# A new order for TensorE in the first attention block, and later due times in the planner that writes it out

## The chip, the core and the metric

The kernel runs on one core of a Trainium2 chip, as one launch. The metric is device microseconds (us) from the launch's start to its end, the median of a few runs. A profile is one execution, recorded instruction by instruction by the hardware. The engines are TensorE (PE; its weight loads are PEld), VectorE (DVE), ScalarE (ACT) and GpSimd (POOL); SyncE (SP) issues nearly all transfers (DMA). Each engine works through its own instructions in the order in which they were written; semaphores tie the engines together.

## The reference

Two attention blocks with inputs of their own, results side by side. Both have 2048 rows, width 512, 32 heads of 16. Block A sees a sliding window of 256 keys, block B all keys.

```python
def _A_ref(x, wqkv, wo):          # _B_ref: the same without the mask
    qkv = (x @ wqkv).reshape(B, S, 3, H, Dh) -> q, k, v   # H = 32, Dh = 16
    scores = einsum("bhqd,bhkd->bhqk", q, k) * (Dh ** -0.5)
    mask = (i - j >= 0) & (i - j < 256)
    scores = where(mask, scores, -1e9)
    o = einsum("bhqk,bhkd->bhqd", softmax(scores), v)
    return concat_heads(o) @ wo
return concatenate([a, b], axis=-1)                # (1, 2048, 1024)
```

All is float32. The kernel reaches that accuracy with two rounded float32 tiles per operand, a rounded value and what it left over, and three products of them.

## The kernel before

**Units.** The work is cut into units (block, group of 4 heads, chunk of 512 queries): 8 groups by 4 chunks make 32 units in each block, numbered 0 to 31 for A and 32 on for B. Unit 19 is group 4, chunk 3 of A.

**The letters.** In block A the order of TensorE is a string, `ORDER_A`, one letter for one step:
- `p`: one projection, 12 matmuls with 128x512 results (`products`, L173), of queries or keys (`project_qk`) or values (`project_v`). ScalarE takes the result out of PSUM (L232, L236 or L312); for queries and keys VectorE or GpSimd makes the two parts (L242, L246, L247), SP stores them to DRAM (L254), and per group they are loaded again as `oq` (L300) and `opk` (L284). There are two store buffers for queries and keys and two for values. The projections of both blocks lie in this string, 96 of them.
- `m`: scores of two heads against a window of 384 keys (L407, 2 matmuls), for the row maximum alone. VectorE copies the masked part and takes the maximum (L416, L417); in the first two query tiles of chunk 0 it does so in another form (L412). Two PSUM buffers serve all m. A unit has 8 m; after the last one `max_finish` makes the negated maxima in three parts (L444 to L447 on VectorE).
- `t`: a transpose of those maxima (L455). ScalarE copies them out (L457) and its own queue sends them into three rows of `oq` (L462).
- `s`: scores of two heads, now less the maximum (L488); ScalarE takes the exponential out of PSUM (L495), GpSimd zeroes the masked corners (L505). A unit has 6 s. Three PSUM buffers serve s, shared with p.
- `w`: exponentials times values (L534), 3 per unit; after the last ScalarE copies the sums out (L545) and SP stores them (L552).
- `e`: maxima for the first unit of block B, against keys loaded early into the buffer of the values (L359; loads L376 and L384).

**The loads.** `load_split` loads a tile of x or of a weight through SP (L141) into a staging buffer. Later ScalarE copies it rounded (L126) and GpSimd, or VectorE for the first tiles, subtracts that from the original (L127). Tiles of the kind "stage" (all of block B, and weights of A but the first) have three staging buffers. A load is written when its condition holds and the planner finds its source ready.

**The planner.** `Model` keeps a time for each engine, for SP and for the transfers, and is run along while the instructions are written. It costs nothing on the chip: its times decide only in which order instructions stand in their engines' programs. The loop over `ORDER_A` asks for each letter when its operands are ready on that clock, and moves the clock there. What other engines do later is put off by `after(time, f)` and written when TensorE's model time passes that time (`settle`); `at_most` and `follow` write it earlier where a buffer or an operand asks for it. `LAND` is added to some of those times for transfers to arrive. `operands` says when a projection may start: its tiles split, and a store buffer free by the time it ends. `invert_now` loads the sums of a chunk (L566), takes reciprocals on VectorE (L571) and stores them (L573), for both blocks.

**Block B** follows a short pattern, `ORDER`, with 16 key tiles for each unit, paced by a fixed step; the same planner places its loads and output projections.

Of the kernel before, what the change touches and what calls it, by code (L numbers as in the profile page):

```python
# [50 lines left out]


ORDER_A = (
    "pppppppmmpmmpmpmpmmpmtmmpmsmmpmsmppmmtpmsmswsmmspmmswwspsmwtsmmpmswmmspsmmwsmptmmpsmmswmspmmspmmswsm"
    "mswtmmspmmswsmpsmwsmtmwmspmsmwsmpmsmwstmwmspsmmpmsmwspmsmwtsmpmmswsmpmsmwsmpmsmtwmsmpsmmswsmmpsmsmws"
    "wtmmspsmmwsmpsmmwsmtpsmmswmsmwsmptpmsmwswmmspmsmwmspmspmswsmsmtwmmspsmmwsmpsmmwstmwmsmpmswmssmmssmmt"
    "mwmsmsmwsmwmssmmswsmtmsmwmsmsmwsmpmmwsmmswsmtmpsmwmsmmswmmsmtpssmmpwstmsmmwmsmswsmmstwspwssmpmsmwmsm"
    "swmsmswmsmsmpmmwmtmswmmssmwsmsmpmsmwsmsmtwmsmpsmmtwspmmswsmwwsmmpsmwtmsmpmmswspmswmsmpmsmtwspsmwmspm"
    "smwsmpswsmmpmsmswtmmspsmwmsmpsmwsmmtpmswmsmwsmpeswespmswmmspeswsmmpmswtemspesmpesmpmsmwsmwsempesmwtm"
    "spesmwsmpestmwsmmpmsmwsmpeswmswemspemspesmtwsepmsmwsmpmswsempmsmwsmptmmwsmpmsmpwmmpsmmpmswsmmpmsmpsm"  # L60
    "mpmmpmmwwtpmm")
LAND = 700


class Model:
# [41 lines left out]
def attention_kernel(ctx: ExitStack, tc: tile.TileContext, xT, wqk, wv, wo, out):  # L107
# [9 lines left out]
    M = Model()  # L117
    ready = {}
# [11 lines left out]
    slots_st, slots_v = [0, 0], [0, 0]  # L130
    staged = {"stage": [0] * 3, "p": [0] * 2 * AHEAD}

    def load_split(srcs, tags, d, keys, stage):

        slots = staged[stage]
        bufs_in = 3 if stage == "stage" else 2 * AHEAD
        at_most(stage, bufs_in - 1)
        r = sb.tile([128, 512] if stage == "stage" else [128, 2, QC], F32, name=f"in_{keys[0]}".translate(NAMES),
                    tag=stage, bufs=bufs_in)
        r = r[:, None] if stage == "stage" else r[:, 0:len(keys)]  # L140
        nc.sync.dma_start(r, srcs)  # L141
        t = M.dma(256 * len(keys), slots.pop(0))

        def rest():
            for n, (tag, key) in enumerate(zip(tags, keys)):
                d[key] = split(r[:, n], tag[0], f"{key}".translate(NAMES), tag[1],
                               nc.gpsimd if stage == "stage" else nc.vector)
                ready[tag[0], *key] = M.run(*(("Pool", 1260) if stage == "stage" else ("DVE", 602)),
                                            M.run("ACT", 500, t))
            slots.append(ready[tag[0], *key])  # L150
        after(t + (LAND if stage == "stage" else 0), rest, (stage, *keys[0]))

    def load_x(b, c, i, n=1):
        load_split(xT[b][128 * i:128 * (i + n), c * QC:(c + 1) * QC].rearrange("(n p) t -> p n t", n=n),
# [267 lines left out]
    def max_finish(b, g, c):  # L422

        n = f"{b}_{g}_{c}"
        eng = nc.gpsimd if slot[0] else nc.vector
        m = mt[b, g, c]
        if b == 0:
            mr = m[:, :, :, 0]
        else:
            mm = sb.tile([128, HG, 4], F32, name=f"mm_{n}", tag="mm")  # L430
            nc.vector.tensor_reduce(out=mm, in_=m, axis=AX.X, op=ALU.max)
            mr = mm

        nm = sb.tile([128, 2, 3, HG // 2, 4], BF16, name=f"nm_{n}", tag="nm")
        parts["nm"] = nm
        nm = [nm[:, :, i].rearrange("p a r q -> p a (r q)") for i in range(3)]
        r1 = sb.tile([128, HG, 4], F32, name=f"nr_{n}", tag="nr")
        mr, r1 = (x.rearrange("p (a r) q -> p a (r q)", a=2) for x in (mr, r1))
        if slot[0]:
            eng.tensor_scalar(mr, mr, -1.0, None, op0=ALU.mult)  # L440
            eng.tensor_copy(nm[0], mr)
            eng.tensor_sub(r1, mr, nm[0])
        else:
            nc.vector.tensor_scalar(nm[0], mr, -1.0, None, op0=ALU.mult)  # L444
            nc.vector.scalar_tensor_tensor(r1, mr, -1.0, nm[0], op0=ALU.mult, op1=ALU.subtract)
        eng.tensor_copy(nm[1], r1)
        eng.tensor_sub(nm[2], r1, nm[1])  # L447
        ready["nm", b, g, c] = M.run("DVE", 1200 if b else 1000)

    def max_rows(b, g, c):  # L450
        n = f"{b}_{g}_{c}"
# [109 lines left out]
    def invert_now(b, p, c, t):  # L561

        n = f"{b}_{p}_{c}"
        at_most("sums", 1)
        ld = sb.tile([128, 32], F32, name=f"ld_{n}", tag="ld")
        nc.sync.dma_start(ld, heads(b, p, c)[:, :, DH])  # L566
        t = M.dma(16, t) + 2000
        rd = sb.tile([128, 32], F32, name=f"rd_{n}", tag="rd")

        def rest():  # L570
            nc.vector.reciprocal(rd, ld)  # L571
# [491 lines left out]
```

## Time and profile before

| | us |
|---|---|
| median of 3 runs | 1947.02 |
| lowest, highest | 1943.77, 1948.77 |
| the profiled execution | 1940.28 |
| its span, first to last instruction | 1938.6 |
| TensorE busy (matmul) in the span | 1884.3 (97%) |
| VectorE, ScalarE, GpSimd busy | 1547.9, 1411.6, 470.7 |
| mean granted TensorE clock | 0.981 |

The span lies 1.7 us under the time of its own execution, and that time 6.7 us under the median of the runs. The page cuts the span into 40 slices of 48.5 us; a digit is the busy share in tenths, and PEclk the clock that the throttle granted to TensorE, 9 for nearly full. Block A and all projections take up the first 12 to 13 slices; the rest is block B, whose last slices hold the final output projections. In a row of the timeline stand start, length, engine, line, operation, tiles, a count of merged instructions, and in brackets how long the engine was idle before it and what ended that. In a row by stretches stand each engine's busy time with its number of instructions, TensorE's granted clock, the transfers' share and their GB/s.

### The profile page before, as it was taken

Reading aid. Unit: us, or ns where it says so; the run is one execution under the profiler, and the core shown is the slowest. Engines: PE = TensorE matmul, PEld = TensorE weight load, DVE = VectorE, ACT = ScalarE, POOL = GpSimd, SP = SyncE. Lnnn points to the kernel's source line nnn. Section 1 sums busy time; section 2 is a strip of 40 time slices with the busy share of each in tenths; the row PEclk is TensorE's granted clock in tenths of the full one; section 3 lists DMA queues with packets and bytes.
Section 4 is the critical chain, followed back from the end, with each engine's and each line's share of the span. In section 5 each row is a group of like instructions: output and inputs, shape, how many; then the busy total and the mean of one; then the engine's idle time right before and its main releaser. Section 6 shows DMA issues by size and latency. Waiting matters only on the chain.

```text
span 1938.6 us, 37511 instructions
## 1 busy us (share of the span) xinstructions
PE 1884.3 (97%) x14464; PEld 942.6 (49%) x14464; DVE 1547.9 (80%) x2320; ACT 1411.6 (73%) x2754; POOL 470.7 (24%) x896
## 2 busy tenths in 40 slices
PE   8999988999999999999999999999999999999998
PEld 5666645566665444444444444444444444444444
DVE  5566566655768867699999999999999999999700
ACT  4355555555545766688888888888888888988763
POOL 0257676633674322001000000100000001010010
PEclk9999978999999999999999999999999999999999
DMA  8655655445555222411130031121031130010111
GB/s 250 161 175 166 200 158 176 135 136 148 172 179 151 69 78 90 102 31 27 35 64 15 16 77 34 39 60 29 16 71 33 27 78 17 29 37 19 40 40 60
DMA packets 129139, 166.71 MB, mean 86 GB/s; under 512 B 22996, under 2 KB 58836, under 8 KB 128948
## 3 DMA queue, kind: packets, MB, share of 16 engines
q1 hardware_dynamic: 127232, 163.52, 29.4%
q8 instruction: 114, 1.87, 0.4%
q10 hardware_dynamic: 1728, 0.79, 0.2%
q14 instruction: 65, 0.53, 0.1%
HBM read 94.49 MB, written 68.19 MB: 84 GB/s over the span
## 4 chain that ended last, share of the span: by engine, by line
PE 87%; DMA 4%; issue 3%; DVE 2%; ACT 2%; POOL 1%; SPq 1%; ACTq 0%; DVEq 0%; POOLq 0%
PE ps_all L519 27%; PE ps_all L359 19%; PE ps_all L488 18%; PE ps_all L173 16%; PE ps_all L534 4%; PE ps_all L407 3%; ACT p L495 1%; DMA oq<-ntr 1%; DVE mt L417 1%; DMA in<-xT_A 1%; PE ps_all L455 1%; DVE ps_all L416 0%; DMA in<-xT_B 0%; DVE mt L363 0%; DMA parts<-st 0%
## 5 line engine op out<-in xcount | busy, mean ns | idle before, releaser
L495 ACT ACTIVATE p<-ps_all 128x512 f32<-128x512 f32 x2432 | 1266.5, 595 | 215.9 <-PE ps_all L488 130.2
L363 DVE TENSOR_REDUCE mt<-ps_all 128x2 f32<-128x1024 f32 x1516 | 1204.7, 872 | 105.6 <-PE ps_all L359 53.6
L488 PE MATMUL ps_all<-oq,opk 51*128 51x512 f32 (+2 forms) x2752 | 797.0, 414 | 13.4 <-ACT p L495 8.5
L359 PE MATMUL ps_all<-opk,oq 48*128 48x512 f32 x2016 | 677.8, 439 | 2.2 <-DVE mt L363 2.1
L519 PE MATMUL ps_all<-p,vt 128*32 128x256 f32 (+1 forms) x6144 | 600.3, 463 | 0.0
L488 PEld LDWEIGHTS ps_all<-oq,opk 51*128 51x128 f32 x2752 | 401.9, 187 | 224.5 <-ACT p L495 186.2
L359 PEld LDWEIGHTS ps_all<-opk,oq 48*128 48x128 f32 x2016 | 312.5, 185 | 325.6 <-DVE mt L363 145.0
L505 POOL TENSOR_SCALAR_AFFINE_SELECT p<-p 128x256 f32<-128x256 f32 x480 | 180.4, 408 | 232.7 <-ACT p L495 232.1
L519 PEld LDWEIGHTS ps_all<-p,vt 128*32 128x32 f32 x6144 | 121.2, 108 | 221.6 <-issue 212.1
L173 PE MATMUL ps_all<-x,w 128*128 128x512 f32 x768 | 198.1, 408 | 6.7 <-ACT x L126 6.3
L440 POOL TENSOR_SCALAR mm<-mm 128x16 f32<-128x16 f32 x31 | 7.8, 253 | 796.5 <-PE ps_all L488 538.3
L416 DVE COPY_PREDICATED ps_all<-mone,ps_all 128x256 f32<-128x256 uint16 x224 | 94.9, 424 | 113.5 <-PE ps_all L407 112.6
L173 PEld LDWEIGHTS ps_all<-x,w 128*128 128x128 f32 x768 | 142.8, 192 | 48.4 <-ACT x L126 7.0
L417 DVE TENSOR_REDUCE mt<-ps_all 128x2 f32<-128x512 f32 x224 | 155.2, 693 | 7.7
L605 POOL TENSOR_TENSOR t<-t,bl 128x512 f32<-128x512 f32 x31 | 39.8, 1283 | 316.7 <-DMA bl<-rl 170.5
L407 PE MATMUL ps_all<-opk,oq 48*128 48x384 f32 (+2 forms) x512 | 99.3, 392 | 14.6 <-DVE mt L417 7.6
L173 PE MATMUL ps_all<-w_o,x_o 128*128 128x512 f32 x384 | 98.9, 410 | 7.5 <-ACT x_o L126 5.4
L534 PE MATMUL ps_all<-p,vt 128*32 128x384 f32 (+2 forms) x1408 | 103.9, 410 | 0.4 <-POOL p L505 0.4
L236 ACT ACTIVATE raw<-ps_all 128x512 f32<-128x512 f32 x56 | 33.5, 598 | 96.2 <-PE ps_all L173 90.0
L173 PE MATMUL ps_all<-w_v,x 128*128 128x512 f32 x384 | 98.3, 406 | 0.0
L173 PEld LDWEIGHTS ps_all<-w_o,x_o 128*128 128x128 f32 x384 | 72.6, 195 | 31.9 <-ACT x_o L126 5.9
L173 PEld LDWEIGHTS ps_all<-w_v,x 128*128 128x128 f32 x384 | 71.5, 192 | 19.5 <-issue 1.7
(58 smaller groups left out, 627.0 us busy)
## 6 DMA issues: line engine op xcount, KB each, us to landing
parts<-st SPq DMA_DIRECT2D x64, 512.0 KB
opk<-parts SPq DMA_DIRECT2D x128, 128.0 KB
oq<-parts SPq DMA_DIRECT2D x128, 128.0 KB
od<-ou SPq DMA_DIRECT2D x64, 256.0 KB
vd<-vst SPq DMA_DIRECT2D x32, 272.0 KB
opk<-parts SPq DMA_DIRECT2D x128, 64.0 KB
oq<-parts SPq DMA_DIRECT2D x128, 64.0 KB
t<-od SPq DMA_DIRECT2D x32, 256.0 KB
```

What stands on the lines that cost most here:

```text
L173: nc.tensor.matmul(ps, l(u), r(v), start=start and k == 0, stop=stop and k == n - 1)
L359: nc.tensor.matmul(ps[:, n], q[rows, 128 * qt:128 * qt + 128], k[rows, kc * QC:kc * QC + QC], start=True, stop=True)
L363: nc.vector.tensor_reduce(out=m[:, a:a + len(heads), r, qt, kc], in_=ps, axis=AX.X, op=ALU.max)
L407: nc.tensor.matmul(two[:, a, 0:w], opq[b, g, c][rows, r, 128 * qt:128 * qt + 128], opk2(g)[rows, r, t0:t1], start=True, stop=True)
L416: nc.vector.copy_predicated(two[:, :, 256:384], later, two[:, :, 0:128])
L417: nc.vector.tensor_reduce(out=m[:, :, r, qt, 0], in_=two[:, :, 128:384], axis=AX.X, op=ALU.max)
L488: nc.tensor.matmul(ps[x][:, col:col + n1], opk2(g)[rows, pr, 128 * k:128 * k + 128], opq[b, g, c][rows, pr, q0:q0 + n1], start=True, stop= ...
L495: nc.scalar.activation(p[:, a0 + x, :w], ps[x][:, :w], AF.Exp, scale=SCALE)
L505: nc.gpsimd.affine_select(out=v, in_=v, pattern=[[0, 2], [sign, 128]], compare_op=ALU.is_ge, fill=zero_fill, base=base, channel_multiplier ...
L519: nc.tensor.matmul(o[32 * j:32 * j + 32, q0:q1], vt[(g // 2) % 2][:, kt, vc:vc + 32], pts[1, g, c, kt, j // 2][:, j % 2, q0:q1], start=kt ...
L534: nc.tensor.matmul(o[32 * j:32 * j + 32, q0:q0 + w], vt[(g // 2) % 2][:, kt, vc:vc + 32], pts[b, g, c, m, j // 2][:, j % 2, col:col + w], ...
L605: nc.gpsimd.tensor_mul(t, t, bl)
```

## The change

The string `ORDER_A` is replaced by another with the same number of each letter; a first landing time, `LAND`, is joined by two more:
- `LAND_X` = 3500 in place of 700 for tiles of the kind "stage": ScalarE's copy and the subtraction are written that much after the model's landing.
- `LAND_V` = 2000: a projection waits on the model's clock until its store buffer has been free that much longer.
- the sums that `invert_now` loads count as landed after 4000 in place of 2000.
- the four VectorE steps of `max_finish` count as 1360 ns, in place of 1000 in block A and 1200 in block B.

No instruction is added or removed; what can differ is where each stands in its engine's or queue's order.

```diff
 ORDER_A = (
-    "pppppppmmpmmpmpmpmmpmtmmpmsmmpmsmppmmtpmsmswsmmspmmswwspsmwtsmmpmswmmspsmmwsmptmmpsmmswmspmmspmmswsm"
-    "mswtmmspmmswsmpsmwsmtmwmspmsmwsmpmsmwstmwmspsmmpmsmwspmsmwtsmpmmswsmpmsmwsmpmsmtwmsmpsmmswsmmpsmsmws"
-    "wtmmspsmmwsmpsmmwsmtpsmmswmsmwsmptpmsmwswmmspmsmwmspmspmswsmsmtwmmspsmmwsmpsmmwstmwmsmpmswmssmmssmmt"
-    "mwmsmsmwsmwmssmmswsmtmsmwmsmsmwsmpmmwsmmswsmtmpsmwmsmmswmmsmtpssmmpwstmsmmwmsmswsmmstwspwssmpmsmwmsm"
-    "swmsmswmsmsmpmmwmtmswmmssmwsmsmpmsmwsmsmtwmsmpsmmtwspmmswsmwwsmmpsmwtmsmpmmswspmswmsmpmsmtwspsmwmspm"
-    "smwsmpswsmmpmsmswtmmspsmwmsmpsmwsmmtpmswmsmwsmpeswespmswmmspeswsmmpmswtemspesmpesmpmsmwsmwsempesmwtm"
-    "spesmwsmpestmwsmmpmsmwsmpeswmswemspemspesmtwsepmsmwsmpmswsempmsmwsmptmmwsmpmsmpwmmpsmmpmswsmmpmsmpsm"
-    "mpmmpmmwwtpmm")
+    "ppppppmmmmpppmmpmmpptmmmpmssmmspmmppmmtpswmsmpmsmwswsmmpmswtmmspmsmwmspmmspmswtmmpmsmswsmmpsmpmsmwsm"
+    "mstwmmspmswmmspmsmwstwsmmpmswsmmpmmswstmwmspmsmpsmwmsmpsmwtmmspmswsmsmpmsmpstwmsmwmspmwmssmmpmswsmms"
+    "twmmspmmswsmpmsmwtmspmswmsmwsmpmmspsmwmsmtwsmpsmwspsmmpsmmwswstmmspmmssmwmsmpsmwmtmwsmmpsmsmwmsmstmm"
+    "swmsmmswmswmmsmswmsmswsmtmsmwmmspsmsmwmmswmstmpsmwmmssmwsmtmmpmsswmsmtmpmsmwsmwsmspswmsswstpmsmmwsws"
+    "msmmswmsmmpmmswmssmwmtsmmwmspmsmwsmsmmswsmtmpmsmtwmsmpsmwsmwwmsmpswtmmspmmswsmpmswmmspsmwtmmspmmswsp"
+    "mswsmpmsmspmswsmmpmmswsmwtmsmpmswtsmpsmmwswmsmpsewmsmpmswsempsewsmpsewtmmspsempesmpmmswmswsempsewtes"
+    "mpmsmwmspemswtsmmpmswsmmpesmwswemspsempsmwtemspeswesmpmmswsmmpmswsmmpmsmwtpmmpswmmspmmpsmwmsmpmmswmp"
+    "smmpmmpwmmtpm")
 LAND = 700
+LAND_V = 2000
+LAND_X = 3500
...
-        after(t + (LAND if stage == "stage" else 0), rest, (stage, *keys[0]))
+        after(t + (LAND_X if stage == "stage" else 0), rest, (stage, *keys[0]))
...
-        ready["nm", b, g, c] = M.run("DVE", 1200 if b else 1000)
+        ready["nm", b, g, c] = M.run("DVE", 1360)
...
-        t = M.dma(16, t) + 2000
+        t = M.dma(16, t) + 4000
...
-            t = slots_st[0] - 2700
+            t = slots_st[0] - 2700 + LAND_V
...
-            t = slots_v[0] - 2700
+            t = slots_v[0] - 2700 + LAND_V
```

More of the change, by code (lines that the diff above doesn't have):

```diff
@@ L53 @@
 ORDER_A = (
-    "pppppppmmpmmpmpmpmmpmtmmpmsmmpmsmppmmtpmsmswsmmspmmswwspsmwtsmmpmswmmspsmmwsmptmmpsmmswmspmmspmmswsm"
-    "mswtmmspmmswsmpsmwsmtmwmspmsmwsmpmsmwstmwmspsmmpmsmwspmsmwtsmpmmswsmpmsmwsmpmsmtwmsmpsmmswsmmpsmsmws"
-    "wtmmspsmmwsmpsmmwsmtpsmmswmsmwsmptpmsmwswmmspmsmwmspmspmswsmsmtwmmspsmmwsmpsmmwstmwmsmpmswmssmmssmmt"
-    "mwmsmsmwsmwmssmmswsmtmsmwmsmsmwsmpmmwsmmswsmtmpsmwmsmmswmmsmtpssmmpwstmsmmwmsmswsmmstwspwssmpmsmwmsm"
-    "swmsmswmsmsmpmmwmtmswmmssmwsmsmpmsmwsmsmtwmsmpsmmtwspmmswsmwwsmmpsmwtmsmpmmswspmswmsmpmsmtwspsmwmspm"
-    "smwsmpswsmmpmsmswtmmspsmwmsmpsmwsmmtpmswmsmwsmpeswespmswmmspeswsmmpmswtemspesmpesmpmsmwsmwsempesmwtm"
-    "spesmwsmpestmwsmmpmsmwsmpeswmswemspemspesmtwsepmsmwsmpmswsempmsmwsmptmmwsmpmsmpwmmpsmmpmswsmmpmsmpsm"
-    "mpmmpmmwwtpmm")
+    "ppppppmmmmpppmmpmmpptmmmpmssmmspmmppmmtpswmsmpmsmwswsmmpmswtmmspmsmwmspmmspmswtmmpmsmswsmmpsmpmsmwsm"
+    "mstwmmspmswmmspmsmwstwsmmpmswsmmpmmswstmwmspmsmpsmwmsmpsmwtmmspmswsmsmpmsmpstwmsmwmspmwmssmmpmswsmms"
+    "twmmspmmswsmpmsmwtmspmswmsmwsmpmmspsmwmsmtwsmpsmwspsmmpsmmwswstmmspmmssmwmsmpsmwmtmwsmmpsmsmwmsmstmm"
+    "swmsmmswmswmmsmswmsmswsmtmsmwmmspsmsmwmmswmstmpsmwmmssmwsmtmmpmsswmsmtmpmsmwsmwsmspswmsswstpmsmmwsws"
+    "msmmswmsmmpmmswmssmwmtsmmwmspmsmwsmsmmswsmtmpmsmtwmspmsmwsmwwmsmpswtmmspmmswsmpmswmmspsmwtmmspmmswsp"
+    "mswsmpmsmspmswsmmpmmswsmwtmsmpmswtsmpsmmwswmsmpsewmsmpmswsempsewsmpsewtmmspsempesmpmmswmswsempsewtes"
+    "mpmsmwmspemswtsmmpmswsmmpesmwswemspsempsmwtemspeswesmpmmswsmmpmswsmmpmsmwtpmmpswmmspmmpsmwmsmpmmswmp"
+    "smmpmmpwmmtpm")
 LAND = 700
+LAND_V = 2000
+LAND_X = 3500
 class Model:
```

## The prediction

> **What bounds the kernel now.** I read the page first: the span, the slices, the chain.
>
> ```profile
> span 1938.6 us, 37511 instructions
> PE   8999988999999999999999999999999999999998
> PEclk9999978999999999999999999999999999999999
> PE 87%; DMA 4%; issue 3%; DVE 2%; ACT 2%; POOL 1%; SPq 1%; ACTq 0%; DVEq 0%; POOLq 0%
> ```
>
> TensorE carries 87% of the chain. In slices 5 to 7 (about 240 to 390 us) it is less busy, and there alone its granted clock is low too. Busy time by stretches splits the first block (0 to 610 us) from the second:
>
> ```profile
> core 0: us, PE busy (x) PEld busy (x) DVE busy (x) ACT busy (x) POOL busy (x), PEclk, DMA share, GB/s
> 0.00:610.00 610.00, 567.46 (x3916) 369.64 (x3916) 384.30 (x801) 312.62 (x616) 333.92 (x644) 0.95 0.57 171
> 610.00:1939.00 1329.00, 1316.86 (x10552) 572.92 (x10548) 1163.57 (x1519) 1098.98 (x2138) 136.81 (x252) 1.00 0.18 47
> ```
>
> ```profile
> 250.00:300.00 50.00, 42.44 (x313) 24.10 (x305) 34.91 (x80) 28.30 (x58) 35.78 (x67) 0.76 0.51 152
> 300.00:350.00 50.00, 42.61 (x283) 26.10 (x281) 27.28 (x66) 27.52 (x57) 33.46 (x60) 0.83 0.62 184
> ```
>
> The first block idles TensorE for 610 - 567.46 = 42.5 us, and at a mean clock of 0.95 loses another 0.05 x 610 = 30.5 us. These 73 us are all that a better order can win. The second block idles 12 us; the change touches it only through the landing time in `invert_now` (a reciprocal written later) and the maxima's due time, and with TensorE full there I book nothing. Over a quarter of the 73 us falls into 250:300 (7.6 idle and 0.24 x 50 = 12.0 by the clock = 19.6) and another 16 into 300:350 (7.4 and 8.5).
>
> The prices of the letters come from the timeline of TensorE at full clock, start to next start:
>
> ```profile
> 124.42 0.61 PE L407 MATMUL ps_all<-opk,oq 48*128 48x384 f32 x4
> 124.87 0.40 PE L488 MATMUL ps_all<-oq,opk 51*128 51x384 f32 x4
> ...
> 126.54 0.39 PE L407 MATMUL ps_all<-opk,oq 48*128 48x384 f32 x2
> 126.86 3.00 PE L173 MATMUL ps_all<-x,w 128*128 128x512 f32 x12
> 129.79 0.50 PE L488 MATMUL ps_all<-oq,opk 51*128 51x384 f32 x4
> 130.12 0.39 PE L407 MATMUL ps_all<-opk,oq 48*128 48x384 f32 x2
> 130.44 1.07 PE L534 MATMUL ps_all<-p,vt 128*32 128x256 f32 x16
> 131.44 0.51 PE L488 MATMUL ps_all<-oq,opk 51*128 51x384 f32 x4
> ```
>
> So p costs 2.93 us, s 0.33, m 0.32, w 1.00. Two m side by side cost 0.45, not 0.64: a change of kind costs about 0.19. The letters are the same in number in both strings (280 m, 192 s, 96 p, 96 w, 33 t, 16 e); only waits, changes of kind and the clock can move the time.
>
> **Part 1: landing time for x and w (LAND_X).** Counting TensorE's loads along the old string puts unit 19 (group 4, chunk 3) at 315 to 343.5 us:
>
> ```profile
> 328.91 0.63 ACT L126 ACTIVATE x<-in 128x512 fp32r<-128x512 f32 x1 [3.28 <-DMA in<-xT_B]
> 329.86 0.90 PE L488 MATMUL ps_all<-oq,opk 51*128 51x128 f32 x3 [1.61 <-ACT p L495]
> 334.65 0.30 PE L455 MATMUL ps_all<-ident,nm 128*48 128x128 bf16 x1 [2.45 <-DVE nm L447]
> 315.00:343.50 28.50, 23.14 (x138) 13.44 (x139) 12.95 (x27) 12.61 (x28) 14.97 (x27) 0.70 0.73 212
>   DMA in<-xT_B: 9.6, 4
> ```
>
> ScalarE reaches the copy of an x tile that has not landed and stands for 3.28 us; behind it wait the exponentials that free the score banks, and TensorE waits 1.61 us for one of them. Then a t, written right after the unit's last m and one s, waits 2.45 us for the maxima. The stretch loses 28.5 - 23.14 = 5.4 us idle and 0.30 x 28.5 = 8.6 us by the clock: 13.9. Two things here go. LAND_X writes copy and subtraction 2.8 us of model time later, nearly one p (2.93), and four such waits total 9.6 us, the longest 3.28, so at most about half a microsecond of each stays. And the new string puts m, s, s, w, s ahead of that t: 3 x 0.33 + 1.00 = 2.0 us of TensorE work between the last m and t in place of 0.33. I take back 10.5 of the 13.9 and leave 3.4 for what is late next, the maxima. Bounds: 0, if the transfer is late by as much again, and 13.9.
>
> What moves with the copy: GpSimd's subtraction behind it, the freeing of the staging buffer, and through that the next load on SP's queue.
>
> ```profile
> L126 ACT ACTIVATE x<-in x16: 621/632/635, 255.9 to 348.7; 128x512 fp32r<-128x512 f32 x16
> ```
>
> Sixteen x tiles in 92.8 us is 6.2 us each. A buffer is held for landing (some 3.3 us by the wait above), 0.63 of copy and about 1.3 of subtraction, then 2.8 more: 8 us, and there are three, so one comes free every 2.7 us. The delay hides behind 6.2; if that cover went, each tile could cost 2.8.
>
> [...]
>
> ```profile
> 395.00:400.00 5.00, 2.97 (x25) 1.96 (x27) 1.96 (x9) 1.57 (x3) 1.44 (x4) 1.00 0.78 235
> 463.02 0.56 PE L359 MATMUL ps_all<-vt,qe 48*128 48x512 f32 x1 [2.42 <-DMA vt<-parts]
> 465.00:470.00 5.00, 5.00 (x27) 3.02 (x28) 2.04 (x2) 2.04 (x4) 1.47 (x4) 0.50 0.51 148
> ```
>
> About 2.0 us without work in 395 to 400 kept the clock at 1.00; a gap of 2.42 was followed by 0.50. So gaps of 2 to 2.5 us decide, and taking 1.61 and 2.45 away should bring the clock back. [...]
>
> **Part 2: where VectorE cannot keep up.** An m needs a copy and a maximum on VectorE:
>
> ```profile
> L417 DVE TENSOR_REDUCE mt<-ps_all 128x2 f32<-128x512 f32 x92 | 63.8, 693 | 3.2
> L416 DVE COPY_PREDICATED ps_all<-mone,ps_all 128x256 f32<-128x256 uint16 x92 | 38.9, 423 | 40.4 <-PE ps_all L407 40.0
> L446 DVE CAST nm<-nr 128x16 bf16<-128x16 f32 x14 | 5.4, 384 | 0.5
> L412 DVE CUSTOM_DVE_ANT_0 junk<-ps_all,wmask 128x256 bf16<-128x256 f32 x12 | 5.1, 425 | 4.0 <-PE ps_all L407 2.3 <-DVE mt L412 0.2
> L447 DVE TENSOR_TENSOR nm<-nr,nm 128x16 bf16<-128x16 f32 x14 | 4.2, 302 | 0.5
> L445 DVE SCALAR_TENSOR_TENSOR nr<-mt,nm 128x16 f32<-128x16 f32 x13 | 4.1, 312 | 0.4
> L444 DVE TENSOR_SCALAR nm<-mt 128x16 bf16<-128x16 f32 x13 | 4.0, 311 | 0.4
> L412 DVE CUSTOM_DVE_ANT_0 junk<-ps_all,wmask 128x128 bf16<-128x128 f32 x14 | 4.0, 288 | 18.4 <-PE ps_all L407 15.9 <-PE ps_all L488 1.5
> ```
>
> A unit of a later chunk asks 8 x 1.116 + 1.31 (L444 to L447) = 10.2 us of VectorE. A unit of chunk 0 does half its m by L412: 4 x 1.116 + 4 x 0.425 + 4 x 0.288 + 1.31 = 8.6, and some more for reading the accumulators. With only two banks for m, TensorE must have that much other work in the unit. Units 15 and 16 have no p in either string: unit 15 has 8 m, 5 s, 3 w, t = 7.4 us before and 8 m, 6 s, 3 w, t = 7.7 after; unit 16 comes to 7.0 and 7.7. They lack 2 to 3 us each both times: 0, with 4 us either way, since where the clock falls is not in the string. Unit 20 (group 5, chunk 0) loses its one p: 8 m, 6 s, 3 w = 7.5 us after, lacking 1.1 or more; m beside s is cheaper than priced, so I say 2, and 1.5 for a part of a window at half clock: +3.5. Bounds: 0 (the waits stay short), and 250:300's whole loss, +19.6.
>
> Units 21 and 22 gain a p (three for two):
>
> ```profile
> 365.00:370.00 5.00, 3.52 (x38) 2.00 (x34) 4.76 (x10) 4.53 (x10) 4.48 (x10) 1.00 0.12 41
> 370.00:375.00 5.00, 4.83 (x14) 3.50 (x14) 2.17 (x5) 0.72 (x2) 1.57 (x5) 0.66 0.31 116
> ```
>
> They lose 1.5 idle and 0.34 x 5 = 1.7 by the clock: 3.2. I take back 2.5 (0 to 3.2).
>
> **Part 3: the start.**
>
> ```profile
> 29.02 0.30 PE L407 MATMUL ps_all<-opk,oq 48*128 48x128 f32 x1 [1.02 <-DMA oq<-parts]
> 30.21 0.41 PE L407 MATMUL ps_all<-opk,oq 48*128 48x128 f32 x3 [0.89 <-DMA oq<-parts]
> 218.91 0.35 DVE L571 RECIPROCAL rd<-ld 128x32 f32<-128x32 f32 x1 [5.97 <-DMA ld<-od]
> ```
>
> The old string has seven p ahead of the first m, and both heads' q still come 1.02 and 0.89 us late. The new has six, then four m in a row: if q lands when it did, TensorE idles 2.9 us more, and half a clock window on top makes +4.4. LAND_V puts the third and fourth p later on the model's clock, so SP may issue q ahead of two stores and win all 1.9 back. I take +2, nearer the row of today, since the store and the load of q still come from the second p.
>
> **Part 4: small ones.** VectorE's 5.97 us wait for the sums at 218.91 goes with 4000 in place of 2000, and some waits of GpSimd for its store buffer with LAND_V; TensorE felt little of them: -1 (0 to -2). Changes of kind rise from 392 to 399: 7 x 0.19 = +1.3. The wait for early keys at 463.02 stays: between the last w of unit 23 and the first e lie 3 p, 3 w, 6 s and 9 m before, 3 p, 3 w, 7 s and 8 m after; 0 (-6 if its 2.4 and the half clock after it go, +2).
>
> **Sum:** -10.5 + 3.5 - 2.5 + 2 - 1 + 1.3 = -7.2 us. Against the profiled execution (span 1938.6, 1940.3 in all) that is 1933.1; its time lies 6.7 under the median of 1947.0, so on the median 1939.8.
>
> **Rivals.** (a) The wait moves along. If SP issues x later by what the copy moved, unit 19 keeps its 13.9: -7.2 + 10.5 = +3.3, 1950.3. For it: the constants only reorder, they make no transfer faster. Against: a slot every 2.7 us for a need of 6.2.
> (b) Slower: unit 20. A unit without p falls behind VectorE, the gap passes 2 to 2.5 us, the clock halves and, as in 250:300, stays low over several windows. That costs 19.6 in place of 3.5: -7.2 + 16.1 = +8.9, 1955.9. It decides from a loss of 10.7 us in unit 20, where the gain is gone. For it: the string there, and units 15 and 16 now. Against: unit 20 lacks less than they do, and a halved TensorE lets VectorE catch up.
> (c) Much faster: clock kept in units 15 to 19 as well. Taking 12 of the clock's 12.0 + 8.5 us in 250:350 beside what is booked gives -19, 1928. Against: units 15 and 16 lack as before.
>
> **Chances.** Forecast 0.42, (a) 0.20, (b) 0.26, (c) 0.12. About 0.3% (5.8 us) is what a measurement of this kernel can tell from none. The forecast's own spread (gain of 3 to 13) puts four fifths over that: faster 0.34 + 0.12 = 0.46; same 0.20 + 0.08 = 0.28; slower 0.26. The range from 1927 to 1954 holds the forecast, (a), nearly half of (c) and a part of (b); for the forecast alone it would be 1934 to 1944.
>
> **What would show it.** Right: in the first block TensorE idle under 40 us and clock at 0.96 or more; the waits of ScalarE for xT_B well under 9.6 us; no t waiting 2 us near unit 19; some 2 us of idle in unit 20. Wrong: a clock under 0.85 around unit 20 (b); waits for xT_B as long as before (a); more than 4 us lost ahead of the first m; a second block that differs by over 1 us, of which nothing here gives a cause.

## The result and the profile after

The changed kernel takes 1957.52 us (median of 6 runs, 1953.19 to 1958.23) against 1946.22 for the kernel before on the same chip (6 runs, 1941.99 to 1951.55): ratio 1.0049 (95% interval 1.0025 to 1.0073), some 9.5 us slower by the ratio. The profiled executions lie further apart, 1958.23 us (span 1956.5) against 1940.28 (span 1938.6), since that of before was at the fast end of its kernel's runs. The new lines after the constants shift the line numbers by 2: L409 is what L407 was, L490 L488, L446 L444.

The page of the changed kernel, span, slices and chain:

```profile
span 1956.5 us, 37507 instructions
PE   7899989889999999999999999999999999999998
PEclk8899988799999999999999999999999999999999
PE 90%; DMA 4%; DVE 3%; ACT 1%; SPq 1%; issue 1%; ACTq 0%; POOL 0%; DVEq 0%
```

VectorE went from 2% to 3% of the chain, and the clock now dips in the first two slices as well. Busy time by stretches, after; the first block ends at 624 in place of 601 us:

```profile
0.00:628.00 628.00, 574.54 (x3900) 376.10 (x3900) 385.28 (x797) 309.81 (x611) 332.86 (x644) 0.93 0.54 165
...
0.00:50.00 50.00, 37.59 (x145) 28.85 (x146) 22.33 (x48) 19.36 (x33) 3.38 (x14) 0.90 0.72 222
50.00:100.00 50.00, 44.76 (x250) 30.69 (x252) 26.78 (x59) 16.65 (x35) 8.32 (x22) 0.90 0.55 145
...
350.00:400.00 50.00, 43.46 (x315) 26.27 (x308) 33.96 (x72) 27.74 (x55) 34.02 (x67) 0.83 0.39 125
400.00:450.00 50.00, 44.41 (x322) 29.28 (x321) 26.22 (x65) 22.92 (x46) 16.37 (x39) 0.93 0.43 127
```

The same four stretches before:

```profile
0.00:50.00 50.00, 40.06 (x167) 29.35 (x167) 26.91 (x59) 20.50 (x36) 3.38 (x14) 1.00 0.80 245
50.00:100.00 50.00, 45.88 (x286) 31.14 (x287) 29.30 (x60) 20.62 (x42) 13.71 (x32) 0.97 0.65 167
350.00:400.00 50.00, 44.20 (x362) 27.77 (x366) 35.60 (x78) 27.82 (x57) 31.08 (x64) 0.97 0.51 156
400.00:450.00 50.00, 49.26 (x378) 32.60 (x373) 29.10 (x69) 28.14 (x55) 20.55 (x50) 1.00 0.39 116
```

At 0 to 100 and 350 to 450 both busy time and clock fell. In the first 628 us TensorE idles 53.5 us now and loses 0.07 x 628 = 44 us by the clock.

To find the letters, I measure each unit from its first m to the next unit's first m and take off the price of its letters (TensorE's own start-to-start times at full clock in the trace of before). What is left is the unit's excess: idle time and half clock. A wait ahead of a unit's first m counts to the unit before it. After against before, in us:

| place | before | after | change |
|---|---|---|---|
| first m | 29.0 | 30.8 | +1.8 |
| units 0, 1 | 8.2 | 14.0 | +5.8 |
| units 2 to 10 | 5.2 | 6.6 | +1.4 |
| unit 11 | 0.9 | 4.7 | +3.8 |
| units 12 to 18 | 25.6 | 27.1 | +1.5 |
| unit 19 | 12.9 | 9.4 | -3.5 |
| unit 20 | 2.0 | 3.1 | +1.1 |
| unit 21 | 2.7 | 8.6 | +5.9 |
| unit 22 | 4.5 | 2.6 | -1.9 |
| unit 24 | 0.1 | 6.2 | +6.1 |
| unit 28 | 0.3 | 4.1 | +3.8 |
| all others of A | 11.5 | 10.1 | -1.4 |

The sum, 24.4, is close to TensorE's later end of the first block (624.4 for 600.6). The span grew by 17.9 only, so the second block came back 5 to 6 us shorter.

The table rests on one execution of each kernel, and executions differ. Up to unit 20 the instructions of e9 and e16 (both below) are those of the kernel before, and those of e11 are the changed kernel's. The first m of unit 20 stands at 343.6 us before, but at 349.8 in e9 and 351.3 in e16; it stands at 359.0 after and 355.6 in e11. Reckoned again in the same way, units 0 and 1 come to 8.5 us before, 10.6 in e9, 10.9 in e16, 14.2 after and 13.5 in e11; unit 24 comes to 0.3 before and to 3.4 in e9. So a single row is sure to some 3 us, the profile before flatters its kernel, and the start's loss is nearer 4 us than the 7.6 of the first two rows.

Most of the loss stands in three kinds of place: the start, the change of group (units 11 and 24), and unit 21. Unit 28 is none. In both kernels a wait for early keys in unit 27 is followed by 6.8 us at half clock, from 463.2 us before and from 488.0 after. Before, all of that fell into unit 27; after, most of it falls into unit 28:

```profile
486.00 0.47 PE L361 MATMUL ps_all<-vt,qe 48*128 48x512 f32 x1 [1.71 <-DMA vt<-parts]
```

Reckoned again, units 27 and 28 together come to 5.9 us before and 6.6 after. The waits of TensorE after:

```profile
PE ps_all L409 <- DMA oq<-parts: 12.1, 5, 5.9
```

TensorE waited 12.1 us for q in five places; before, it was 6.4 in five, the longest 2.0.

### The profile page after: what moved, and what is told of

Its sections match the earlier page's. It is cut to its first block, busy times and chain, and to the rows that moved or that the text cites. A ratio compares the mean times of both kernels' runs of the same rounds, so it can differ in the third digit from the quotient of the medians.

```text
span 1956.5 us, 37507 instructions
## 1 busy us (share of the span) xinstructions
PE 1893.2 (97%) x14464; PEld 949.5 (49%) x14464; DVE 1552.9 (79%) x2320; ACT 1411.7 (72%) x2754; POOL 469.8 (24%) x896
## 4 chain that ended last, share of the span: by engine, by line
PE 90%; DMA 4%; DVE 3%; ACT 1%; SPq 1%; issue 1%; ACTq 0%; POOL 0%; DVEq 0%
PE ps_all L521 28%; PE ps_all L361 19%; PE ps_all L490 18%; PE ps_all L175 17%; PE ps_all L536 4%; PE ps_all L409 3%; DMA oq<-parts 1%; DVE mt L419 1%; ACT p L497 1%; DMA oq<-ntr 1%; PE ps_all L457 1%; DVE ps_all L418 1%; DMA od<-ou 0%; DMA opk<-parts 0%; DVE nm L446 0%
## 5 line engine op out<-in xcount | busy, mean ns | idle before, releaser
L490 PE MATMUL ps_all<-oq,opk 51*128 51x512 f32 (+2 forms) x2752 | 795.0, 414 | 14.0 <-ACT p L497 10.0
L521 PE MATMUL ps_all<-p,vt 128*32 128x256 f32 (+1 forms) x6144 | 600.6, 463 | 0.2 <-ACT ou L547 0.2
L490 PEld LDWEIGHTS ps_all<-oq,opk 51*128 51x128 f32 x2752 | 402.2, 188 | 219.2 <-ACT p L497 185.9
L361 PEld LDWEIGHTS ps_all<-opk,oq 48*128 48x128 f32 x2016 | 312.6, 185 | 327.0 <-issue 145.3
L409 PE MATMUL ps_all<-opk,oq 48*128 48x384 f32 (+2 forms) x512 | 104.3, 406 | 26.8 <-DMA oq<-parts 12.1
L175 PE MATMUL ps_all<-w_v,x 128*128 128x512 f32 x384 | 103.7, 424 | 0.0
L409 PEld LDWEIGHTS ps_all<-opk,oq 48*128 48x128 f32 x512 | 53.5, 198 | 70.9 <-issue 27.9
L175 PEld LDWEIGHTS ps_all<-w_v,x 128*128 128x128 f32 x384 | 75.8, 203 | 21.3 <-issue 2.4
```

The costliest lines, as they stand in the source:

```text
L175: nc.tensor.matmul(ps, l(u), r(v), start=start and k == 0, stop=stop and k == n - 1)
L361: nc.tensor.matmul(ps[:, n], q[rows, 128 * qt:128 * qt + 128], k[rows, kc * QC:kc * QC + QC], start=True, stop=True)
L409: nc.tensor.matmul(two[:, a, 0:w], opq[b, g, c][rows, r, 128 * qt:128 * qt + 128], opk2(g)[rows, r, t0:t1], start=True, stop=True)
L490: nc.tensor.matmul(ps[x][:, col:col + n1], opk2(g)[rows, pr, 128 * k:128 * k + 128], opq[b, g, c][rows, pr, q0:q0 + n1], start=True, stop= ...
L521: nc.tensor.matmul(o[32 * j:32 * j + 32, q0:q1], vt[(g // 2) % 2][:, kt, vc:vc + 32], pts[1, g, c, kt, j // 2][:, j % 2, q0:q1], start=kt ...
```

## The experiments

Each ratio is against the kernel before, run on the same chip in the same rounds, with its 95% interval.

### Times or string: e1, e2

e1 has the new due times with the old string, e2 the new string with the old times.

> The changed kernel's due times with the old string. Theory T (the due times reorder the transfers: at the start two loads of x, 1 MB, now stand ahead of the first q on SP's queue, and later key loads ahead of other q): this alone is slower, by 3 to 8 us, and the first m waits for q till about 30.5 us instead of 29.0. Rival S (the letters are to blame: the first m one p earlier, unit 20 without p, units 11 and 24 asking for q too early): this is as fast as before or, since ScalarE no longer stands for x tiles, up to 8 us faster, 1938 to 1947.

> The new string with the due times of before. Theory T: near before, at most +4 us, from the first m that stands one p earlier (idle till 29.0 us instead of 5.9 us till 30.8). Rival S: slower by as much as the change, +8 to +15, with waits for q near the first m of units 0, 12 and 24 as in the changed kernel. If both parts carry it together, +5 to +8.

e1: 0.9972 (0.9948 to 0.9997). e2: 1.0011 (0.9990 to 1.0033). The times alone gain a little, as rival S of e1 had it; the string alone is level to slightly slower, as theory T of e2 had it. Together they are slower than either, so they work on each other.

### The start: e3, e4, e15

e3 is the changed kernel with the old first 45 letters; e4 the kernel before with the new ones:

```diff
-pppppppmmpmmpmpmpmmpmtmmpmsmmpmsmppmmtpmsmsws   (old)
+ppppppmmmmpppmmpmmpptmmmpmssmmspmmppmmtpswmsm   (new)
```

> The changed kernel, but the first 45 letters (to about 75 us) as before; both strings have used the same letters there. In the profiles the changed kernel is 9.1 us behind at that letter and keeps that. If the start's loss is its own, this gains 6 to 9 us: 1948 to 1952. If what follows only waits for the same transfers later, it gains under 2.

> The kernel before with the new string's first 45 letters and all due times of before. Theory T: q lands at 29.0 us as before, TensorE idles 4 us from 25.0, one window at half clock: +4 to +6. Rival S: the letters alone cost the 9 us of the start: +9.

e3: 1.0023 (1.0000 to 1.0045) in place of 1.0049; these two intervals overlap, so the 5 us between them are not sure. e4: 1.0068 (1.0045 to 1.0091): the new start in front of the old body is the costliest of all, more than either expectation. In its profile TensorE is 11.4 us late after unit 4 and stays so (15.2 at the end of the first block); against e9, which has the same letters but the old start, it is 8.6 and 7.4. In the changed kernel's timeline of TensorE the two long gaps of the start are:

```profile
30.84 3.04 PE L409 MATMUL ps_all<-opk,oq 48*128 48x128 f32 x8 [5.88 <-DMA oq<-parts]
63.37 0.90 PE L490 MATMUL ps_all<-oq,opk 51*128 51x384 f32 x4 [2.77 <-DMA oq<-ntr]
```

The first m waits 5.88 us for q where two waits of 1.02 and 0.89 stood. One p (2.9 us) that stood ahead of it now stands behind. q itself also lands 1 to 2 us later: LAND_V changes the order of SP's queue, so that two loads of x stand directly ahead of the first load of q. SP's queue after, then before:

```profile
21.42 0.94 SPq L143 DMA_DIRECT2D in<-xT_A  x2
22.40 2.63 SPq L302 DMA_DIRECT2D oq<-parts  x4
```

```profile
17.21 1.39 SPq L141 DMA_DIRECT2D in<-xT_A  x2
...
23.20 3.28 SPq L300 DMA_DIRECT2D oq<-parts  x4
```

SP issues q 0.8 us earlier than before, and still q lands later. e5 below, with the old string and LAND_V 0, has its first m at 29.1 us; e1, which differs in LAND_V 2000 alone, at 30.9. In the twelve profiles without LAND_V the first m starts at 28.8 to 30.2 us, in the seven with it at 30.1 to 31.5.

e15 puts that p back in e4:

```diff
-ppppppmmmmpppmm
+pppppppmmmmppmm
```

> The kernel before with the new first 45 letters (ratio 1.0068, 11.4 us late after unit 4), but the p that stands after the first four m is moved ahead of them, as the old string has it. Theory: the start's loss begins with the first m's wait for q (3.8 us, TensorE idle) and the half clock behind it; with a p in that gap some 3 to 6 us come back: ratio 1.003 to 1.005. Rival: the loss is the letters after it (maxima bunched where keys and vst are not there yet): 1.006 to 1.007.

e15: 1.0057 (1.0036 to 1.0079), against 1.0068; the difference lies within the intervals. Its timeline of TensorE:

```profile
29.52 0.29 PE L407 MATMUL ps_all<-opk,oq 48*128 48x128 f32 x1 [1.22 <-DMA oq<-parts]
...
59.97 0.90 PE L488 MATMUL ps_all<-oq,opk 51*128 51x384 f32 x4 [3.51 <-DMA oq<-ntr]
```

The wait for q fell from 3.77 to 1.22 us as expected, but the first s's wait for the transposed maxima rose from 2.85 to 3.51, and units 1 to 4 lost no less than in e4. That rise says little by itself: with the old start the same wait was 1.93 us before, 2.74 in e16 and 4.63 in e9. But one p ahead of the first m did not bring the 3 to 6 us, so the run goes with the rival: most of the start's loss sits in the letters behind the first m. Which of them no run shows.

### Chunk 0 of a new group: e8

Units 12, 24 and 28 are the first of their groups. SP has 16 key loads of the new group to issue ahead of q (SP's queue in the changed kernel; the lengths hold waits of SP, too):

```profile
395.49 11.36 SPq L286 DMA_DIRECT2D opk<-parts  x12
...
408.87 2.52 SPq L286 DMA_DIRECT2D opk<-parts  x4
...
413.87 4.37 SPq L302 DMA_DIRECT2D oq<-parts  x4
```

TensorE meets them at the first m of unit 24, and again one m on:

```profile
416.79 0.29 PE L409 MATMUL ps_all<-opk,oq 48*128 48x128 f32 x1 [1.38 <-DMA oq<-parts]
420.36 0.66 PE L409 MATMUL ps_all<-opk,oq 48*128 48x128 f32 x3 [3.28 <-DMA od<-ou]
```

Before, q's loads and the first m of unit 24 stood so (SP's queue, then TensorE):

```profile
393.69 3.32 SPq L300 DMA_DIRECT2D oq<-parts  x4
```

```profile
398.92 0.66 PE L407 MATMUL ps_all<-opk,oq 48*128 48x128 f32 x2 [1.96 <-DMA oq<-parts]
```

The first of q's loads began 5.2 us ahead of the m that needs it, and the m waited 1.96 us. In the changed kernel it begins 2.9 us ahead. The releaser od<-ou in the second row of TensorE is the profile's; q's four loads were still being issued until 418.24. e8 is e3 with one p moved ahead of the first m in units 12, 24 and 28:

```diff
-mwsmpmmspsmwms        -smpswtmmspmmsws       -psewmsmpmswse
+mwsmpmpmssmwms        +smpswtpmmsmmsws       +psewmspmmswse
```

> The changed kernel with the old start and with one p moved ahead of the first m of units 12, 24 and 28, where TensorE waited 3.7, 5.0 and 2.8 us for q of a new group. Theory: q of a new group stands on SP behind its sixteen key loads and is asked for 3 to 5 us too early; one p (2.93 us) covers most: 6 to 9 us faster than without the move (1953): 1944 to 1947. Rival: the transfers are late because the engines that feed them are late, and the wait moves along: under 2 us faster.

e8: 1.0003 (0.9988 to 1.0018) against e3's 1.0023: 4 us for three letters, less than the 6 to 9 expected, and the two intervals overlap. In its profile unit 12's first m waits 0.49 us for q where it was 3.49 in e3, and unit 11 comes to 1.4 us where it was 4.5. That place is explained. Unit 24 is not: the 1.38 us ahead of its first m are gone, but on the second m this is left of the 3.28,

```profile
407.12 0.41 PE L409 MATMUL ps_all<-opk,oq 48*128 48x128 f32 x3 [1.58 <-issue]
```

and 6.8 us at half clock follow, as in the changed kernel. Unit 24 comes to 6.5 us in e8, against 5.4 in e3 and 6.4 in the changed kernel. What SP itself waited for ahead of q's loads, in the changed kernel from 385 to 428 us:

```profile
SPq L302 <- DMA oq<-ntr: 2.8, 1, 2.8
SPq L302 <- DMA od<-ou: 2.0, 1, 2.0
```

SP stood 2.8 us ahead of the last of q's four loads, until ScalarE's transfer of unit 23's transposed maxima had landed; the four loads take 4.37 us of its queue there and 4.43 in e8. In the profile before SP has no such wait ahead of unit 24's q. In the old string the t of unit 23 stands behind unit 24's first m, in the new one ahead of it, and e8 leaves it there. So q is late in unit 24 not for its place in the queue alone. Why its load waits for that transfer the views do not say, and no run moves the t by itself.

### The sums at 4000, and part of the times: e5, e6, e7

e5 is e1 with LAND_V 0; e6 is the kernel before with the 4000 alone; e7 has the new times and the new letters from 244 to 466 only (from inside unit 12 to just ahead of unit 24: neither the start nor the late q).

> The old string with the new due times, but LAND_V = 0. With all due times it ran at 0.997 of before: q landed at 30.8 us in place of 29.0 (4 us behind at the 13th letter), and the second block came out 5 us shorter. If LAND_V is what puts two loads of x ahead of the first q, q lands at 29.0 us again, the 4 us are not lost, and it is 2 to 5 us faster than with all of them: 1936 to 1941. If LAND_V also spares ScalarE and GpSimd waits for store buffers that TensorE feels, it is no faster, 1943 or more.

> The kernel before with one due time changed: the sums of a chunk count as landed after 4000 in place of 2000. Theory: it moves the reciprocals and with them the output projections of the last stretch, and alone takes 3 to 5 us out of the second block; the first block as before. 1943 to 1945. If the gain of the second block comes from the maxima's 1360 or from chance, no change.

> New due times; letters 244 to 466 of the new string, the old string before and behind. In the profiles the whole new string (with the old start) falls 12.6 us behind the old one at equal due times: +8.7 up to letter 244, -4.4 from there to 466, +8.3 behind. If these stretches stand for themselves, this is some 4 us faster than the old string with the new due times: 1936 to 1941. If the free-running clock windows or what precedes decides, it falls anywhere from 1936 to 1950.

e5: 0.9984 (0.9967 to 1.0001), no different from e1: q lands early again, but the 2 to 5 us expected of that do not show. e7: 0.9991 (0.9975 to 1.0008): against the kernel before, the middle of the new string with the new times loses nothing that can be measured, though unit 21 stands at 8.7 us in its profile; nor does it gain the 4 us over e1 that were expected. e6: 1.0019 (1.0001 to 1.0036): its second block is 5 us shorter, its first longer, with unit 21's excess at 12.4 us. So did e1 and e5 (11.2, 11.3), and the changed kernel (8.6), and this led to an instruction at unit 21.

### Unit 21: a VectorE instruction held by GpSimd

The changed kernel's timeline of VectorE at the end of unit 20's maxima:

```profile
368.84 0.69 DVE L419 TENSOR_REDUCE mt<-ps_all 128x2 f32<-128x512 f32 x1
369.57 3.50 DVE L446 TENSOR_SCALAR nm<-mt 128x16 bf16<-128x16 f32 x1
```

Sixteen numbers a partition take 3.50 us; the shortest of this line took 0.174. GpSimd at that time:

```profile
365.82 2.92 POOL L507 TENSOR_SCALAR_AFFINE_SELECT p<-p 128x256 f32<-128x256 f32 x8
368.71 1.29 POOL L129 TENSOR_TENSOR w_v<-in_v,w_v 128x512 fp32r<-128x512 f32 x1
369.96 1.84 POOL L507 TENSOR_SCALAR_AFFINE_SELECT p<-p 128x256 f32<-128x256 f32 x5
371.76 1.28 POOL L129 TENSOR_TENSOR w_v<-in_v,w_v 128x512 fp32r<-128x512 f32 x1
376.82 1.12 POOL L507 TENSOR_SCALAR_AFFINE_SELECT p<-p 128x256 f32<-128x256 f32 x3 [3.78 <-ACT p L497]
```

GpSimd runs without a pause until 371.76 + 1.28 = 373.04, and VectorE's instruction ends at 373.07. In e5 the same instruction took 5.81 us:

```profile
357.16 5.81 DVE L446 TENSOR_SCALAR nm<-mt 128x16 bf16<-128x16 f32 x1
```

```profile
356.44 4.71 POOL L507 TENSOR_SCALAR_AFFINE_SELECT p<-p 128x256 f32<-128x256 f32 x13
361.11 1.27 POOL L129 TENSOR_TENSOR w_v<-in_v,w_v 128x512 fp32r<-128x512 f32 x1
362.32 0.62 POOL L248 CAST st<-raw 128x512 fp32r<-128x512 f32 x1
363.01 1.28 POOL L249 TENSOR_TENSOR st<-raw,st 128x512 fp32r<-128x512 f32 x1
```

It ends at 362.97, in the first gap of GpSimd's row of work (362.94 to 363.01). In e6 it took 6.92 us, in e2 one of another unit 5.22, each ending 0.03 us after GpSimd's pause began (at 367.93 and at 321.86). In e3, e7 and e8 it took 3.50 to 3.55. The maxima of the next unit wait behind it on VectorE, TensorE's m waits 2.46 us for them at 374.82, and the clock is at half for 13.7 us from 375.3. The reductions beside it run at their usual 0.69; these read PSUM. Why the one is held and the others are not, no view says. VectorE was held not for one instruction of GpSimd but for all that followed one another without a gap: seven after, fourteen in e6.

e9 keeps the 2000 in the first block; e10 is e5 with the closing maxima of unit 20 on GpSimd, e11 the changed kernel with the same, e12 is e5 with all closing maxima of the first block there.

```diff
-        t = M.dma(16, t) + 2000
+        t = M.dma(16, t) + (4000 if b else 2000)      # e9
...
-        eng = nc.gpsimd if slot[0] else nc.vector
+        on_pool = slot[0] or (b, g, c) == units[20]   # e10, e11; in e12: or b == 0
+        eng = nc.gpsimd if on_pool else nc.vector
...
-        if slot[0]:
+        if on_pool:
```

> The kernel before with the 4000 for the sums in the second block alone (2000 stays in the first). Theory: the 4000 has two effects that the runs so far show together. In the second block it takes 4.6 to 6.1 us off; in the first it moves one of VectorE's small max instructions (the TENSOR_SCALAR of max_finish) to a place where GpSimd runs without a gap, and it is held there 3.5 to 6.9 us (unit 21's excess 8.5 to 12.4 us in every kernel with the 4000, 1.8 to 3.1 in those with 2000). Then this kernel has before's first block (TensorE enters the second block within 2 us of 600.6, no max instruction over 2.2 us) and a second block about 5 us shorter: ratio 0.9975 (0.996 to 0.999). Rival: the 4000 gains in the second block only what a late first block had lost before; then the ratio is 0.9995 to 1.002 and the second block is as long as before's.

> The old string with the new due times but LAND_V 0, and the four closing instructions of one group's maxima (unit 20's, whose TENSOR_SCALAR stood 5.81 us on VectorE) on GpSimd, where they queue behind the run that held them; all else as in that kernel (ratio 0.9984). Theory: VectorE goes on with unit 21's maxima at once, the 5.8 us leave TensorE's path as far as nothing else is late there: unit 21's excess falls from 11.3 to about 5 us, the half clock stretch that follows it goes, ratio about 0.995 to 0.9965. Rival: the instruction was long because something else was late (keys, the half clock), then unit 21's excess stays at 9 us or over and the ratio at 0.998 to 0.999.

> The changed kernel with the same four instructions of unit 20's group on GpSimd (its TENSOR_SCALAR stood 3.50 us on VectorE). Theory: unit 21's excess falls from 8.6 to about 5 us, ratio 1.0049 to about 1.003; the rest of the loss (start, units 11 and 12, 24, 28) stays. Rival: no change of unit 21, ratio 1.005.

> As e10, but the closing instructions of all 33 groups of the first block's maxima on GpSimd. Theory of the held instructions: on these four lines VectorE stood 27.7 us over its own shortest times in the first block with all groups there; TensorE waited for VectorE's maxima 7 to 10 us in all, so at most some 3 us more than e10 are to be had: ratio 0.993 to 0.9965. Rival: GpSimd takes them later than VectorE did and holds back the masks of p and the key products in its queue; the minus-max turns come late: slower than e10 by 2 to 10 us (0.997 to 1.002).

e9: 0.9969 (0.9951 to 0.9986), unit 21 at 2.7 us. Its first block, with the instructions of before, ends about 8 us later than before's, not within the 2 us expected; the gain is in the second block. e10: 0.9946 (0.9926 to 0.9966) against e5's 0.9984, unit 21 from 11.3 to 2.8. e11: 1.0012 (0.9994 to 1.0030) against 1.0049, unit 21 from 8.6 to 1.8. The half clock is gone there (stretch of unit 21 in e11):

```profile
365.10:376.50 11.40, 10.18 (x93) 6.16 (x93) 8.82 (x17) 5.43 (x11) 10.74 (x24) 1.00 0.49 153
```

e12: 1.0002 (0.9985 to 1.0018), in the range of its rival: what one group wins 33 groups lose; its unit 11 went from 0.7 to 7.8 us. That GpSimd finishes the maxima later than VectorE did is the rival's account of it, and no view shows by how much.

The second block's gain in e9 is in TensorE's waits from 1640 us on. Before:

```profile
PE ps_all L173 <- ACT x_o L126: 5.4, 1, 5.4
PE ps_all L173 <- POOL x_o L607: 1.2, 1, 1.2
PE ps_all L173 <- POOL x_o L608: 0.6, 1, 0.6
```

In e9:

```profile
PE ps_all L173 <- ACT x_o L126: 5.3, 1, 5.3
PE ps_all L488 <- ACT p L495: 0.5, 1, 0.5
```

The two waits for GpSimd's part of the last output projections are gone, and the half clock behind them; from a common point its second block is 4.4 us shorter, the changed kernel's 4.6. From TensorE's first product of block B's exponentials and values (L519) to the end it takes 1328.8 to 1333.0 us in the six profiles with 2000 there, and 1324.3 to 1327.0 in twelve of the thirteen with 4000 (e3: 1329.4).

### LAND_X alone, all mended, and a control: e13, e14, e16, e17

e14 is the kernel before with LAND_X 3500 alone; e13 is e8 with unit 20's maxima on GpSimd, so that start, late q and held instruction are all mended; e16 is the kernel before with unit 20's maxima on GpSimd; e17 is e10 with the 4000 in the second block only.

> The kernel before with the landing time of x in split loads at 3500 in place of 700, and nothing else. The prediction booked -10.5 us for this at unit 19. Theory now: unit 19's excess falls only from 12.9 to 9.4 or so, because the half clock of that stretch and p's masks hold TensorE once the x parts are there: -1 to -3.5 us, ratio 0.998 to 0.9995. Rival (the prediction's term holds when the old times stand elsewhere): unit 19's excess falls to 2 to 4 us and the ratio to 0.9945.

> The changed kernel with the old first 45 letters, one p ahead of the first m of units 12, 24 and 28, and unit 20's closing maxima on GpSimd: the three places of the loss mended together. Theory (start, late q, held VectorE instruction are the whole loss, and add up): e8's 1.0003 less what the GpSimd step gave the changed kernel (1.0049 to 1.0012): 0.9966 (0.995 to 0.998), faster than before. Rival: the new letters lose in other units as well once these are mended, and the ratio stays at 0.999 to 1.001.

> The control of e10 and e11: the kernel before with unit 20's closing maxima on GpSimd. In the kernel before this TensorE unit's TENSOR_SCALAR stood 0.29 us on VectorE, it was not held. Theory (the step gains only because it takes a held instruction off VectorE): 0.999 to 1.001, unit 21's excess stays at 2 to 3.5 us. Rival (fewer small instructions on VectorE there, or another order of GpSimd's masks, gain by themselves): 0.996 to 0.998 as e11 against the changed kernel.

> e10 (ratio 0.9946: old string, x at 3500, maxima 1360, LAND_V 0, unit 20's closing maxima on GpSimd) with the 4000 of the sums in the second block alone. Theory: e10's gain is unit 19, unit 22 and the second block's end; the 4000 in the first block adds nothing: 0.994 to 0.996. Rival: the later reciprocals keep VectorE's order right in the first block, and without them another closing instruction is held: 0.997 to 1.000, with a TENSOR_SCALAR or CAST of 3 us or more in the first block.

e14: 1.0016 (0.9996 to 1.0035). Unit 19 fell to 8.8 us, but unit 21 rose to 11.2, with the same instruction at 5.78 us. So it is not the 4000 that makes it be held, as I had written for e9: another shift of some microseconds does it too. In none of the profiles with both old times and the old body (before, e4, e9, e15) was it held, though in the profile before it ran at 356.40 in the middle of thirteen masks of GpSimd and took 0.29. Why it got in there stays open.

e13: 0.9970 (0.9957 to 0.9983), 0.9966 expected: the three steps add up, and more than the loss is gone. That does not make the three places the whole loss. Unit 24 still stands at 4.9 us in e13's profile, and the step to GpSimd is no mending of the new string alone: it gains on the kernel before as well (e16), and with the new times the old string reaches 0.9946 with it (e10, with LAND_V 0). Whether the mended new string is as good as the old one no run shows.

e16: 0.9971 (0.9953 to 0.9990). The control fell: on the kernel before, where the profiled instruction was not held, the step gains as well, as the rival had it. Unit 21 stayed at 2.7 in the profile, unit 22 went from 4.5 to 2.2. So of e11's gain a part would come anywhere; that unit 21's excess went from 8.6 to 1.8 is the part that the profile ties to the held instruction. The times don't separate the two: the step gains 0.38% in e10 against e5, 0.37% in e11 against the changed kernel and 0.29% here, and these are level within their intervals. In the untraced runs of the kernel before it may be held in some; no run here can tell.

e17: 0.9933 (0.9909 to 0.9957), 1934.44 us against 1946.62: the best version of this study, about 12 us faster than before, and faster than the changed kernel. Its interval overlaps e10's, so no gain of the 4000 in the first block shows.

## Why the prediction was wrong

The forecast was 7 us faster; the kernel is some 9.5 slower. Step by step, in the profiles' basis:

- **Part 3, the start (+2)** was mis-sized: first m +1.8, units 0 and 1 another +5.8 in the two profiles, but some 4 in all against e9 and e16, near the bound of +4.4. I priced only q's wait ahead of the first m. The letters behind it lose most of it (e4, e15). SP did issue q earlier, as hoped of LAND_V, but directly behind two loads of x, and q landed later. By the runs the start is worth 0.26% (changed kernel against e3), 5 us, with intervals that overlap.
- **The step that was missing** is q at a change of group, a term that the sum does not have. The prediction counted letters in units 15, 16 and 20 to 22 against VectorE, and never asked in each chunk 0 how far the last p stands from the first m that needs it, nor what SP waits for ahead of q's loads. Unit 11 costs 3.8 us there and unit 24 some 3 to 6 in the profiles. A p moved ahead brought unit 11 back (e8); unit 24 stayed, and its cause is open beyond SP's wait of 2.8 us.
- **Part 4, "-1" for the sums**, and rival (b): a halved clock did come with late maxima, but in unit 21, not 20, and not since a p was missing. VectorE had the time; one instruction of it was held 3.50 us, which the prediction did not foresee. Unit 20 cost 1.1 of the 3.5 booked. Units 21 and 22, booked at -2.5, came to +4.0.
- **Part 1, LAND_X (-10.5)** gave -3.5. The mechanism was half right. ScalarE's waits for x fell from 9.6 us in four to one:

```profile
343.06 0.63 ACT L128 ACTIVATE x<-in 128x512 fp32r<-128x512 f32 x1 [3.10 <-DMA in<-xT_B]
```

```profile
338.65 0.37 SPq L143 DMA_DIRECT2D in<-xT_B  x1
```

  One of 3.10 us is left, where the longest had been 3.28: SP issued that load at 338.65, behind eight key loads that had taken its queue from 330.05 to 338.55 (4.3 us of that a wait for transposed maxima to land), and ScalarE asked for it 1.3 us later. I read this as rival (a), in one tile of four and at the place where it counts; that its staging buffer came free too late is not shown. With the same LAND_X and the old string, three waits of 6.6 and 6.7 us are left in e1 and e5, one of 2.5 in e14. TensorE pays for it with another wait:

```profile
344.02 0.55 PE L490 MATMUL ps_all<-oq,opk 51*128 51x128 f32 x3 [2.84 <-ACT p L497]
```

  With LAND_X alone (e14) the exponentials come in time, and t waits 3.58 us for the maxima in place of 2.45. In the changed kernel the idle time of the unit did not move, 27.10 - 21.71 = 5.4 us; what went is clock, 8.6 to 0.13 x 27.1 = 3.5 us:

```profile
331.90:359.00 27.10, 21.71 (x134) 14.11 (x130) 11.05 (x21) 12.42 (x28) 17.60 (x32) 0.87 0.65 190
```

  The half microsecond per wait that I left was the step that failed, and with it the largest term of the sum.
- **The second block, nothing booked**, gave 4 to 5 us: later reciprocals moved two waits for the last output projections out of the way. The text named over 1 us there as a sign that something was missing, and it was.
- **Changes of kind (+1.3)** were counted and priced by two measures. The count of 392 to 399 takes m, s and e for one kind; the price of 0.19 is that of an m beside another letter. Counted so, neighbours that differ fall from 636 to 628, which would be -1.5. No run separates this term. (The two slices that the prediction calls 5 to 7 end at 339 us, not 390; no term rests on that.)
- **The clock.** That gaps of 2 to 2.5 us decide held only in part. Gaps of 2.46 and 2.84 us were each followed by half clock. But the longest such stretch of the changed kernel, 27.3 us from 279.8, follows four waits of 0.35, 0.83, 0.83 and 0.62 us within 3.7 us, and in e9 a wait of 1.41 at the m where the prediction's row kept its clock after 2.0 was followed by 6.8 us at half clock. So the length of one gap does not decide; what does, no run tests. Nor does a run show the 1.5 us that Parts 2 and 3 add for a part of a window at half clock, in unit 20's +3.5 and in the start's bound of +4.4. In the changed kernel's profile unit 20 (359.0 to 368.5) kept the clock at 1.00, and at the start it stood at half for 10.2 us from 27.2, three windows of 3.41.

## What to carry to other kernels

When an order is searched on a model, check by hand what the model leaves out at each change of group: the queue that a load stands in, what its issue waits for, and how much other work lies between the step that makes an operand and the first that reads it. With the old start, three moved letters and one group's closing maxima on another engine, a loss of 0.5% became a gain of 0.3%. A due time that lets a copy start later can leave one wait nearly as long as before (3.10 us of unit 19's, where the longest had been 3.28), so book the gain from the last tile of the row, not from the mean.

## What the hardware showed beyond expectation

- A VectorE `TENSOR_SCALAR` on 16 numbers a partition took 3.50 to 6.92 us while GpSimd ran 7 to 14 instructions without a gap, and ended within 0.04 us of GpSimd's first pause (after, e2, e5, e6, e14). In the profile before one took 2.10 us, at 585.24, across five. Beside it, `TENSOR_REDUCE` from PSUM ran at its usual 0.69.
- Before and after, the granted clock is either full or half, and it is at half in stretches of 3.41 us or a multiple: 3.41 to 17.07 us before, 3.41 to 27.31 after, but for the last one, which the end of the profile cuts short. In each of the two profiles the starts of these stretches, too, lie whole multiples of 3.41 us apart (57.06 and 261.86 before: 60 of them); the windows of the prediction and of e4 and e7 are these 3.41 us. Counted from the span's start, the starts lie 2.45 us past a multiple before and 3.27 after. The mean granted clock of the kernel before was 0.972 to 0.983 in 35 runs on one chip; twelve runs of one kernel spread over 4 to 20 us, and a single profile of the first block is uncertain by some 8 us (before and e9).
- SP held a load of q back by 2.8 us until a transfer that ScalarE had issued landed (unit 24).
- The control's gain (e16) and the 0.29 us at 356.40 stay unexplained.
